# Two order edges on VectorE: the last Q clip behind an x addition, and a Q weight sum behind a K sink

## The chip, the cores and the metric

One Trainium2 chip, one of its cores. The time is device microseconds (us) of one execution. TensorE is called PE, VectorE DVE, ScalarE ACT, SyncE SP. A run counts as slow when it is over 1.5% above the fastest run of the same kernel; only fast runs are compared.

Each run also records the mean TensorE clock that was granted, as a share of full speed.

## The reference, cut to what matters

```python
# x: 2048 tokens x 1024, bf16; 32 heads of 32; MLP width 3584
q, k, v = heads(layernorm(x) @ wqkv)
phi = lambda t: where(t > 0, t + 1, exp(t)) + 1e-6
num, den = phi(q) @ (phi(k).T @ v), phi(q) @ sum(phi(k))
h   = x + (num / (den + 1e-6)) @ wo
n   = layernorm(h)
h2  = h + (relu(n @ W_gate) * (n @ W_up)) @ W_down
```

## The kernel before: the parts that matter here

The matrix products are split into seven block products each. DVE forms sums of weight blocks and of token blocks for this, PE multiplies, and DVE and ACT combine the results. The 16 token tiles go through the attention output one after another, and the first MLP products are interleaved with the last tiles, on tokens that are already finished. The stretch discussed here lies at 205 to 228 us.

The four sums of a weight, of which the Q weight's second is moved (the profile calls these lines L133 to L136):

```python
def sums():
    nc.vector.tensor_tensor(out=t1, in0=b12, in1=b11, op=ALU.subtract)
    nc.vector.tensor_tensor(out=t2, in0=b22, in1=t1, op=ALU.subtract)   # L134, moved
    nc.vector.tensor_tensor(out=t3, in0=b22, in1=b12, op=ALU.subtract)  # L135, needs no t2
    nc.vector.tensor_tensor(out=t4, in0=b21, in1=t2, op=ALU.subtract)
```

The end of the feature map `phi`: an Exp on ACT, then the clip (L217), which is moved, and a max, both on DVE:

```python
nc.scalar.activation(out=e, in_=dst, func=ACT.Exp, ...)
nc.vector.tensor_scalar(out=e, in0=e, scalar1=1.0, scalar2=PHI_EPS, op0=ALU.min, op1=ALU.add)
nc.vector.tensor_tensor(out=dst, in0=dst, in1=e, op=ALU.max)
```

A token tile's way through attention, with the names that the profile uses (line numbers of the kernel before):

```python
# nd: PE L527 -> PSUM; ACT takes the reciprocal; DVE writes three pieces of o_sb (L534)
# oT: a DMA transposes o_sb
# wo_h, for each half j:
#   PE attn L557;  DVE x_res L560: h = x + attn          <- "the x addition"
#   after both halves, ACT normalizes h into hn
nc.sync.dma_start_transpose(out=hnT[s][i][:, :, r:r + P], in_=st["hn"][:])   # hn_T, L581
# one step later, on DVE, the sums of the hidden state, L117 to L120, which read what that DMA wrote
left_sums(hnT[n // STS], hns[n // STS], slice(...), nc.vector)
```

Then PE multiplies hidden-state sums `hn`, `hs` by gate and up weight sums `tg`, `tu` (L733; the sums are L640, L644, L645, L646).

Of the kernel before, what the change touches and what calls it, by code (L numbers as in the profile page):

```python
# [7 lines left out]
ACT = mybir.ActivationFunctionType  # L8
ALU = mybir.AluOpType
# [6 lines left out]
PHI_EPS = 1e-6  # L16
# [15 lines left out]
def block_kernel(ctx: ExitStack, tc: tile.TileContext, x, wqkv, wo, wg, wu, wd, out, H: int):  # L32
    nc = tc.nc
# [10 lines left out]
    NW = 512  # L44
    NDW = P + HPC
    SW = 512
    NS = S // (2 * SW)
    KH = KC // 2
# [33 lines left out]
    negb = consts.tile([P, 2], FP32, name="negb")  # L82
# [39 lines left out]
    def left_ops(T, S):  # L122
        (a11, a12), (a21, a22) = blocks(T)
        s1, s2, s4 = (v[:] for v in S)
        return a11, a12, s4, a22, s1, s2, a21.bitcast(FP16)

    def right_ops(w, t):

        (b11, b12), (b21, b22) = [[w[:, k * KH:(k + 1) * KH, j * NW:(j + 1) * NW] for j in range(2)] for k in range(2)]
        t1, t2, t4, t3 = t[:, 0], t[:, 1], t[:, 2], b12.bitcast(FP16)  # L130

        def sums():
            nc.vector.tensor_tensor(out=t1, in0=b12, in1=b11, op=ALU.subtract)  # L133
            nc.vector.tensor_tensor(out=t2, in0=b22, in1=t1, op=ALU.subtract)  # L134
            nc.vector.tensor_tensor(out=t3, in0=b22, in1=b12, op=ALU.subtract)  # L135
            nc.vector.tensor_tensor(out=t4, in0=b21, in1=t2, op=ALU.subtract)  # L136

        return (b11, b21, b22, t4, t1, t2, t3), sums

# [66 lines left out]
    def phi_begin(dst, ps, m):  # L206

        if m is None:
            nc.scalar.activation(out=dst, in_=ps[:], func=ACT.Identity, bias=negb[:, 1:2], scale=1.0)
        else:  # L210
            nc.vector.scalar_tensor_tensor(out=dst, in0=ps[:], scalar=1.0 + PHI_EPS, in1=m,
                                           op0=ALU.add, op1=ALU.add)

    def phi_end(dst, e):

        nc.scalar.activation(out=e, in_=dst, func=ACT.Exp, bias=negb[:, 0:1], scale=1.0)
        nc.vector.tensor_scalar(out=e, in0=e, scalar1=1.0, scalar2=PHI_EPS, op0=ALU.min, op1=ALU.add)  # L217
        nc.vector.tensor_tensor(out=dst, in0=dst, in1=e, op=ALU.max)


    order = [(i * HS + s * SW) // P + tt for s in range(NS) for i in range(2) for tt in range(NT)]

# [4 lines left out]
    pspool = psctx.enter_context(tc.tile_pool(name="ps", bufs=1, space=PSUM))  # L227
    with ExitStack() as actx:
        apool = actx.enter_context(tc.tile_pool(name="apool", bufs=1))
        awork = actx.enter_context(tc.tile_pool(name="awork", bufs=2))  # L230
# [9 lines left out]
        def load_x(t):  # L240
            x_sb = bwork.tile([P, D], BF16, tag=("x_res", "oT")[atiles.index(t) % 2], bufs=XB, name="x_sb")
            nc.sync.dma_start(out=x_sb[:], in_=xf[t * P:(t + 1) * P, :])
            x_tiles[t] = x_sb
# [4 lines left out]
        def place(t):  # L248
            i, r = divmod(t * P, HS)
            s, r = divmod(r, SW)  # L250
            return s, i, r
# [13 lines left out]
        def ln_T(t):  # L265
            if t not in x_tiles:
                load_x(t)
            x_sb = x_tiles.pop(t)
            s, i, r = place(t)
            stats = asmall.tile([P, 2, nc.vector.BN_STATS_DIM], FP32, tag="stats", name="stats")  # L270
            for k in range(2):
                nc.vector.bn_stats(out=stats[:, k, :], in_=x_sb[:, k * NW:(k + 1) * NW])  # L272
            mv = asmall.tile([P, nc.vector.BN_AGGR_DIM], FP32, tag="mv", name="mv")
            nc.vector.bn_aggr(out=mv[:], in_=stats[:])
            sm = asmall.tile([P, 3], FP32, tag="sma", name="sma")
            lnv, rstd, nmr = (sm[:, k:k + 1] for k in range(3))
            nc.scalar.activation(out=lnv, in_=mv[:, 1:2], func=ACT.Ln, bias=LN_EPS, scale=1.0)
            nc.scalar.activation(out=rstd, in_=lnv, func=ACT.Exp, scale=-0.5)
            xn = bwork.tile([P, D], BF16, tag="hn", bufs=HB, name="xn")
            if t == atiles[0]:  # L280
                for k in range(2):
                    ks = slice(k * NW, (k + 1) * NW)
                    nc.vector.tensor_scalar(out=xn[:, ks], in0=x_sb[:, ks], scalar1=mv[:, 0:1], scalar2=rstd,
                                            op0=ALU.subtract, op1=ALU.mult)
                transpose_in(t, xn)
                return
            nc.vector.scalar_tensor_tensor(out=nmr, in0=mv[:, 0:1], scalar=-1.0, in1=rstd, op0=ALU.mult, op1=ALU.mult)
            nc.scalar.activation(out=xn[:], in_=x_sb[:], func=ACT.Identity, bias=nmr, scale=rstd)
            if t not in atiles[:PE_T]:
                nc.sync.dma_start_transpose(out=xT[s][i][:, :, r:r + P], in_=xn[:])  # L290
                return
            transpose_in(t, xn)
# [10 lines left out]
        rk, k_sums = right_ops(wk_sb, tk)  # L303
        rv, v_sums = right_ops(wv_sb, tv)
        pk, vs = {}, {}

        def token_unit(u, right, fin):

            s, _, r = place(units[u][0])
            left = left_ops(xT[s], xS[s])  # L310

            def mm(ps, m, v, start):
                for kc in range(KH):
                    nc.tensor.matmul(ps[:], lhsT=left[m - 1][:, kc, r + v * P:r + (v + 1) * P],  # L314
                                     rhs=right[m - 1][:, kc, :], start=(start and kc == 0),
                                     stop=(kc == KH - 1), skip_group_check=True)

            return strassen(pspool, awork, mm, fin)

        def new_pk(t):  # L320
            slot = atiles.index(t) % KC
            pk[t] = wo_mem[:, slot * D:(slot + 1) * D]

        def k_unit(u):
            ready = {}

            def fin(i, j, v, ps, m):
                t = units[u][2 * i + v]
                if not ready.get(t):
                    new_pk(t)  # L330
                phi_begin(pk[t][:, j * NW:(j + 1) * NW], ps, m)
                ready[t] = ready.get(t, 0) + 1
                if ready[t] == 2:
                    e = bwork.tile([P, D], BF16, tag="o_sb", name="e")
                    phi_end(pk[t], e[:])

            return token_unit(u, rk, fin)

        def k_plain(t):
            s, i, r = place(t)  # L340
# [52 lines left out]
        NU = len(units)  # L393
# [36 lines left out]
                    sums_unit(u + 1)  # L430
        sums_unit(0)
        rq, q_sums = right_ops(wq_sb, tq)
        q_sums()
        for t in units[-1]:
            kv_tile(t)
        nc.sync.dma_start(out=wo_sb, in_=wo.rearrange("(kc p) n -> p kc n", p=P))
        for c in range(KC):
            bnk, i = divmod(c, GPB)
            nc.vector.tensor_tensor(out=kvz[:, c, :], in0=kv_ps[bnk][:, i * NDW:(i + 1) * NDW],
                                    in1=mask[:], op=ALU.mult)  # L440
# [6 lines left out]
    def q_unit(s, c):  # L447

        left = left_ops(xT[s], xS[s])
        ready = {}  # L450

        def mm(ps, m, v, start):
            for kc in range(KH):
                nc.tensor.matmul(ps[:], lhsT=rq[m - 1][:, kc, (c + v) * P:(c + v + 1) * P],  # L454
                                 rhs=left[m - 1][:, kc, :], start=(start and kc == 0),
                                 stop=(kc == KH - 1), skip_group_check=True)

        def fin(i, j, v, ps, m):
            pair = pqT[:, j * KH + c:j * KH + c + 2, i * HS + s * SW:i * HS + (s + 1) * SW]
            phi_begin(pair[:, v], ps, m)  # L460
            if v == 1:
                e = qw[-1].tile([P, 2, NW], BF16, tag="e", name="e")
                phi_end(pair, e[:])

        return strassen(pspool, qw[-1], mm, fin, 3, s == NS - 1 and c + 2 == KH)

# [44 lines left out]
    held, added, squared = [], {}, {}  # L511
# [74 lines left out]
    STS = ST // NS  # L586
# [137 lines left out]
    quad_copies = [{} for f in range(NE)]  # L724
# [57 lines left out]
        attn_step(step)  # L782
    with tc.issue_after(added[order[STS], 0].ins):
        late_sums.pop()()
    steps = QSTEPS + STS + LAG[-1] - ready
    for n in range(steps):
        attn_step(ready + n)
        for p in flow[n * len(flow) // steps:(n + 1) * len(flow) // steps]:
            p()
    for t, copy in ((order[-2], ("m1", 1)), (order[-1], ("u3", 1))):  # L790
        tc.add_manual_dep(squared[t].ins, quad_copies[2][copy].ins.name,
                          mybir.DependencyInfo(mybir.DependencyClass.NoSync, mybir.DependencyReason.DATA),
                          reason="order")
    pqctx.close()
    psctx.close()
    abctx.close()
# [130 lines left out]
    for r, (wt, f, fi, toks) in enumerate(runs):  # L927
        w = [ops() for _, ops in now]
        later = []
        for n, s in enumerate(toks):  # L930
            first = n == 0 and isinstance(wt, int) and fi == 0
# [50 lines left out]
            if k == nwin - 3:  # L982
                for x in range(2):
                    t = wpools[1].tile([P, KC * 2 * GP * P], BF16, tag=("wg", "wu")[x], name="wd")
# [16 lines left out]
    for n in range(2):  # L1001
        t = fpool.tile([P, 4 * D], BF16, tag="wraw", bufs=2, name="xd")
# [247 lines left out]
    for n in range(1, len(OUTER)):  # L1250
        op = ops[n]
# [72 lines left out]
        else:  # L1324
            pss = []
            for p in range(4):
                ps = acc(("A", "A", "XY"[(n + 1) % 2], "XY"[n % 2])[p])
# [12 lines left out]
                s, t0 = divmod(2 * p, NT)  # L1340
                ts = slice(t0, t0 + 2)
                v = ps[:].rearrange("p (t d) -> p t d", t=2)
# [53 lines left out]
```

## Time and profile before

| | before |
|---|---|
| time, first three runs | 737.68 us (737.57 to 738.51) |
| span of the profiled run | 737.2 us (that run took 739.01 us) |
| PE busy in the span | 722.7 us |
| PE idle between 205 and 228 us | 1.94 us |

First the DVE timeline of the kernel before (start us, duration us, engine, line, operation; a bracket gives idle time ahead and what ended it):

```profile
214.95 0.42 DVE L640 TENSOR_TENSOR tg<-wg 128x512 f16<-128x512 bf16 x1
...
216.07 0.96 DVE L534 TENSOR_TENSOR o_sb<-nd,rd 128x384 bf16<-128x384 f32 x2
216.94 0.68 DVE L560 SCALAR_TENSOR_TENSOR x_res<-attn,x_res 128x512 bf16<-128x512 f32 x1
...
217.55 0.42 DVE L117 TENSOR_TENSOR hs<-hn 128x512 f16<-128x512 bf16 x1
```

Then SP's timeline of the DMA that feeds that L117, and the list of DMA issues of the stretch, whose last number is the median time in us from issue to landing:

```profile
213.02 1.23 SPq L581 DMA_TRANSPOSE hn<-hn  x1
```

```profile
hn<-hn SPq DMA_TRANSPOSE x1, 4.4
```

The transfer lands at about 213.02 + 4.4 = 217.4 us, and the sum that reads it starts at 217.55. It needed no wait, by about 0.1 us.

PE's timeline of the kernel before in the same stretch (start us, duration us, engine, line, operation; a bracket gives idle time ahead and what ended it):

```profile
216.62 0.75 PE L527 MATMUL nd<-kvz,pq_mem 128*128 128x132 bf16 x8
...
219.50 1.04 PE L733 MATMUL Aq<-hs,tg 128*128 128x512 f16 x4 [0.41 <-DVE tg L644]
...
221.83 3.40 PE L557 MATMUL attn<-wo_mem,oT 128*128 128x512 bf16 x14
```

`nd` of tile 12 runs through without a wait, and the next `attn` starts at 221.83 us.

### The profile page before, as it was taken

How to read it: one execution, taken by the hardware profiler on the slowest of the kernel's cores; microseconds unless marked ns; L12 is line 12 of the kernel's file. 1: busy time of each engine (PE TensorE's matmuls, PEld its weight loads, DVE VectorE, ACT ScalarE, POOL GpSimd, SP SyncE). 2: the span in 40 equal slices, each digit the busy share in tenths (PEclk: the TensorE clock that was granted, in tenths of full speed). 3: DMA queues.
4: the chain of work that ended last, by engine and by line, in shares of the span. 5: the costliest groups of instructions: out<-in, count | busy, mean ns of one | idle time of the engine just before them, and what ended most of it. 6: DMA issues, size and time to landing. Idle time of an engine off the chain costs nothing.

```text
span 737.2 us, 10549 instructions
## 1 busy us (share of the span) xinstructions
PE 722.7 (98%) x3967; PEld 381.8 (52%) x4020; DVE 556.0 (75%) x980; ACT 321.5 (44%) x580; POOL 20.7 (3%) x56
## 2 busy tenths in 40 slices
PE   8999999999989999999999999999999999999997
PEld 3444555444444444444444444444444458888667
DVE  6997644676789767688768787887786479996677
ACT  4776553778786655444344444443444120000000
POOL 0000000000000000000000000000000001100210
PEclk9999999999999999999999999999999999999999
DMA  9765002079977526175638358575483499978932
GB/s 315 169 145 157 0 1 95 21 168 230 215 166 166 135 73 208 43 207 135 196 106 243 114 188 270 182 219 193 162 280 120 137 392 343 305 253 283 257 44 58
DMA packets 143811, 128.88 MB, mean 175 GB/s; under 512 B 50960, under 2 KB 126096, under 8 KB 143760
## 3 DMA queue, kind: packets, MB, share of 16 engines
q1 hardware_dynamic: 136688, 123.30, 55.6%
q0 software_dynamic: 5312, 3.15, 3.4%
q10 hardware_dynamic: 1760, 1.77, 0.7%
q8 instruction: 31, 0.51, 0.3%
q14 instruction: 20, 0.16, 0.1%
HBM read 76.81 MB, written 39.85 MB: 158 GB/s over the span
## 4 chain that ended last, share of the span: by engine, by line
PE 85%; DVE 7%; DMA 4%; ACT 3%; issue 1%; SPq 0%; DVEq 0%; POOL 0%; ACTq 0%
PE accA L832 22%; PE accX L832 8%; PE accY L832 8%; PE accA L1167 8%; PE attn L557 6%; PE Aq L733 4%; PE Aq L314 3%; PE accA L993 3%; PE accX L1167 3%; PE Aq L454 3%; PE accY L1167 2%; PE Eq L314 2%; PE accY L993 2%; PE accX L993 2%; PE Eq L733 2%; DVE stats L272 1%
## 5 line engine op out<-in xcount | busy, mean ns | idle before, releaser
L842 ACT ACTIVATE gu<-gu 128x512 bf16<-128x512 bf16 x72 | 45.4, 630 | 131.3 <-DVE gu L841 131.3
L837 ACT COPY snap<-accA 128x1024 f32<-128x1024 f32 x72 | 72.5, 1008 | 36.5 <-PE accA L832 36.4
L832 PEld LDWEIGHTS <-tg 128*128 128x128 f16 x384 | 37.6, 98 | 45.3
L832 PEld LDWEIGHTS <-tu 128*128 128x128 f16 x384 | 37.6, 98 | 45.3
L557 PE MATMUL attn<-wo_mem,oT 128*128 128x512 bf16 x247 | 57.9, 379 | 2.6 <-DVE o_sb L534 1.3
L841 DVE TENSOR_TENSOR gu<-accY,snap 128x1024 bf16<-128x1024 f32 x36 | 43.9, 1219 | 10.0 <-ACT snap L837 10.0
L832 PE MATMUL accA<-hn,tg 128*128 128x512 f16 (+1 forms) x192 | 49.3, 379 | 0.0
L832 PE MATMUL accA<-hn,tu 128*128 128x512 f16 (+1 forms) x192 | 49.3, 379 | 0.0
L841 DVE TENSOR_TENSOR gu<-accX,snap 128x1024 bf16<-128x1024 f32 x36 | 43.9, 1219 | 6.4 <-PE accX L832 3.7
L154 ACT COPY u<-Aq 128x512 f32<-128x512 f32 x54 | 31.3, 581 | 36.6 <-PE Aq L314 19.3
L1167 PEld LDWEIGHTS <-x 128*128 128x128 f16 (+1 forms) x448 | 43.9, 98 | 5.5
L832 PEld LDWEIGHTS <-wu 128*128 128x128 bf16 x288 | 28.2, 98 | 34.0
L832 PEld LDWEIGHTS <-wg 128*128 128x128 bf16 x288 | 28.2, 98 | 34.0
L557 PEld LDWEIGHTS <-oT 128*128 128x128 bf16 x256 | 24.6, 98 | 32.5 <-issue 4.1
L845 DVE TENSOR_TENSOR hq<-gu 128x512 bf16<-128x512 bf16 x48 | 20.3, 423 | 14.3 <-ACT gu L842 14.2
L314 PEld LDWEIGHTS <-xT 128*128 128x128 bf16 (+1 forms) x192 | 18.6, 98 | 23.6 <-issue 2.3
L534 DVE TENSOR_TENSOR o_sb<-nd,rd 128x384 bf16<-128x384 f32 (+1 forms) x48 | 23.4, 508 | 8.3 <-ACT rd L533 6.1
L1131 POOL DMA_DIRECT2D out_dram<-o x12 | 15.2, 1265 | 508.8 <-DMA h<-h_dram 419.1
L1167 PEld LDWEIGHTS <-xs 128*128 128x128 f16 x280 | 27.4, 98 | 3.2
L560 DVE SCALAR_TENSOR_TENSOR x_res<-attn,x_res 128x512 bf16<-128x512 f32 x32 | 22.0, 686 | 8.6 <-PE attn L557 8.5
L1173 DVE TENSOR_TENSOR snap<-accA,u 128x1024 f32<-128x1024 f32 x16 | 19.5, 1221 | 11.4 <-PE accA L1167 11.3
L993 PEld LDWEIGHTS <-x 128*128 128x128 bf16 (+1 forms) x168 | 16.4, 98 | 19.6
(235 smaller groups left out, 1420.3 us busy)
## 6 DMA issues: line engine op xcount, KB each, us to landing
x<-x_dram SPq DMA_DIRECT2D x17, 896.0 KB, 8.8
x_dram<-hq SPq DMA_DIRECT2D x28, 512.0 KB, 3.2
wg<-in_B_W_gate_dram SPq DMA_DIRECT2D x14, 512.0 KB, 5.1
wu<-in_B_W_up_dram SPq DMA_DIRECT2D x14, 512.0 KB, 7.3
wraw<-in_B_W_down_dram SPq DMA_DIRECT2D x14, 512.0 KB, 4.9
x_dram<-hq SPq DMA_DIRECT2D x28, 256.0 KB, 2.7
t_dram<-wt SPq DMA_DIRECT2D x28, 256.0 KB, 2.2
xd<-x_dram SPq DMA_DIRECT2D x6, 896.0 KB, 6.9
```

The costliest lines, as they stand in the source:

```text
L154: copies[nm, v] = nc.scalar.copy(out=snaps[nm, v], in_=bank[v][:])
L314: nc.tensor.matmul(ps[:], lhsT=left[m - 1][:, kc, r + v * P:r + (v + 1) * P], rhs=right[m - 1][:, kc, :], start=(start and kc == 0), stop= ...
L454: nc.tensor.matmul(ps[:], lhsT=rq[m - 1][:, kc, (c + v) * P:(c + v + 1) * P], rhs=left[m - 1][:, kc, :], start=(start and kc == 0), stop=( ...
L534: nc.vector.tensor_tensor(out=ov[:, c0:c0 + n], in0=ndv[:, :, 0:P].rearrange("p k (h e) -> p k h e", h=HPC), in1=rd[:, 0:n, :].unsqueeze(3 ...
L557: nc.tensor.matmul(ps[:], lhsT=st["oT"][:, c, :], rhs=wo_sb[:, c, j * NW:(j + 1) * NW], start=(c == 0), stop=(c == KC - 1))
L733: nc.tensor.matmul(ps[:], lhsT=w(v, m)[:, kc, :], rhs=left[m - 1][:, kc, :], start=(start and kc == 0), stop=(kc == KH - 1), skip_group_ch ...
L832: nc.tensor.matmul(ps[:, v, :], lhsT=w[v][n - 1][:, kc, :], rhs=left[n - 1][:, kc, :], start=(t is not None and kc == 0), stop=(kc == KH - ...
L837: nc.scalar.copy(out=st[nm][:], in_=halves(st["A"]))
L841: add(out=g[:], in0=halves(st[nm]), in1=st[base][:], op=ALU.add)
L842: nc.scalar.activation(out=g[:, 0, :], in_=g[:, 0, :], func=ACT.Relu)
L993: nc.tensor.matmul(ps[:, t * NW:(t + 1) * NW], lhsT=x_tile(n, s, kh)[:, f, (t0 + t) * P:(t0 + t + 1) * P], rhs=w_tile(n, kh)[:, f, :], sta ...
L1167: nc.tensor.matmul(pv[:, tt, :], lhsT=left(m)[:, f, tt * P:(tt + 1) * P], rhs=right(m)[:, f, :], start=(t is not None and f == 0 and tt % ...
```

## The change

Two constraints for the instruction scheduler (order edges), no instruction more or less. A K unit is the set of seven block products that gives K for four token tiles; a sink is the DVE instruction (L211) that reads a finished product out of PSUM, where the matmuls of this program leave their results. The clip of the last pair of Q columns is to come after the first x addition of attention tile 8, because it made that addition wait. The second sum of the Q weight is to come after the first K sink of the last K unit, because it made an earlier sink wait.

```diff
+    def behind(late, first):
+        tc.add_manual_dep(late.ins, first.ins.name,
+                          mybir.DependencyInfo(mybir.DependencyClass.NoSync, mybir.DependencyReason.DATA),
+                          reason="order")
 ...
-        q_sums()
+        behind(q_sums(), k_begins[NU - 1, 0, 0, 0])          # q_sums returns its second sum
 ...
     with tc.issue_after(added[order[STS], 0].ins):
         late_sums.pop()()
+    behind(q_ends[NS - 1, KH - 2, 1, 0], added[order[STS], 0])   # phi_end returns the clip
```

The rest of the diff records the instructions that these two lines name, and uses `behind` where the same call stood written out.

## The prediction

> **What bounds the kernel now.** I read the page first, then PE's list of waits, then the timeline around the two instructions that the change moves, then the chain of waits there.

> ```profile
> PE 722.7 (98%) x3967; PEld 381.8 (52%) x4020; DVE 556.0 (75%) x980; ACT 321.5 (44%) x580; POOL 20.7 (3%) x56
> PE 85%; DVE 7%; DMA 4%; ACT 3%; issue 1%; SPq 0%; DVEq 0%; POOL 0%; ACTq 0%
> ```

> TensorE (PE) is busy 722.7 of 737.2 us, at full granted clock in all 40 slices, and holds 85% of the chain that ended last. All PE idle is 14.5 us. A change that only reorders VectorE (DVE) can win nothing but part of the idle time that DVE causes inside PE. PE's waits, longest first (total, times, longest):

> ```profile
> PE tp L299 <- DVE xT L300: 1.7, 1, 1.7
> PE attn L557 <- DVE o_sb L534: 1.3, 4, 0.5
> PE spin L400 <- DVE zero L397: 1.2, 1, 1.2
> PE attn L557 <- DVE x_res L560: 0.8, 1, 0.8
> PE nd L527 <- DVE o_sb L534: 0.5, 1, 0.5
> PE Dq L314 <- DVE wo_mem L211: 0.5, 1, 0.5
> ...
> PE Aq L733 <- DVE tg L644: 0.4, 1, 0.4
> ```

> Four of these lie near the moved instructions: `attn` behind the x addition (L560), `nd` behind `o_sb`, `Dq` behind a K sink (L211), and `Aq` behind a gate weight sum (L644). They fall at 212.02, 213.09, 72.26 and 219.50 us. Together they are 0.82 + 0.48 + 0.47 + 0.41 = 2.18 us, 0.3% of the time. That is about the ceiling for both edges.

> [...] the clip below stands 0.94 us at the head of DVE while an addition whose matmuls should be done stands behind it. [...] L134 took 1218 ns here, and it produces fp16 from bf16. [...] the trace has starts 1.13 us apart for two such sums of 1.22 us (L135 at 74.53, L136 at 75.66), so I use start-to-start distances. [...]

> **The change, part by part.** No instruction is added or removed. Each edge tells the instruction scheduler to place one DVE instruction after another on the same engine. The scheduler places instructions by its own estimate of times and by priority, so what it puts in the hole is the open question.

> *Edge A: the clip.* DVE before, with start, duration, instruction, and idle before it:

> ```profile
> 209.58 0.42 DVE L120 TENSOR_TENSOR hs<-hn,hs 128x512 f16<-128x512 bf16 x1
> 210.93 0.43 DVE L217 TENSOR_SCALAR e<-e 128x1024 bf16<-128x1024 bf16 x1 [0.94 <-ACT e L216]
> 211.28 0.69 DVE L560 SCALAR_TENSOR_TENSOR x_res<-attn,x_res 128x512 bf16<-128x512 f32 x1
> 211.88 0.09 DVE L560 DVE_READ_ACCUMULATOR x_res<-attn,x_res 128x1 f32 x1
> 211.88 0.69 DVE L218 TENSOR_TENSOR pq_mem<-pq_mem,e 128x1024 bf16<-128x1024 bf16 x1
> 212.49 0.55 DVE L534 TENSOR_TENSOR o_sb<-nd,rd 128x384 bf16<-128x384 f32 x1
> ```

> Counting the sixteen pairs of L560 in time order, the one at 211.28 is the first half of the ninth tile, index 8: just the one that the edge names. The clip ahead of it waits for an Exp that ScalarE started only at 209.76 (1.14 us long), because a Square and two copies came first. The matmuls of that half start at 207.59; eight at about 0.216 us end near 209.32, plus some 0.2 us to the wake-up. So the addition could start at about 209.92, straight after L120, and not at 211.28: 1.36 us sooner. Its result frees the PSUM buffer for which PE stands idle from 211.20 to 212.02. PE itself cannot use all of the 1.36 us: the 16 matmuls of tile 8 occupy it until about 207.59 + 16 x 0.216 = 211.04. The start at 212.02 can move to about 211.04.

> It then meets the next wait. The clip's Exp is still ready only at 210.93. If the clip and its max follow straight after the addition, clip 210.93, max 211.27, `o_sb` 211.87: all as before less the 0.61 us that the addition no longer spends behind the clip. So `nd`, which waits for `o_sb`, moves from 213.09 to about 212.48, and part of the 0.82 us reappears there: the two idles of 1.30 us become one of about 0.8 or 0.9. From 210.93 to past 219 DVE is nearly gapless (8.90 busy of 9 us from 211 to 220), so the whole queue up to L644 shifts by the same 0.6 us, and so does PE's start at 219.50. If other ready work fills the hole too, the shift can reach the full 0.94 us of removed stall; if L644 is also placed sooner, its 0.41 us is on top. After 219.50 PE is full to 249.4 and most of what it waits for is fed by PE itself, so the shift should stay. **Edge A: about 0.7 us gained** (0.6 plus a little for better filling).

> The late clip should harm nobody: the part of Q it completes is first read by the score matmuls of tile 12, which begin at 216.62, over 4 us later.

> *Edge B: the weight sum.* The Q weight's second sum (L134) now sits in the K unit before the last:

> ```profile
> 69.79 0.68 DVE L117 TENSOR_TENSOR xS<-xT 128x1024 f16<-128x1024 bf16 x1
> 70.39 1.22 DVE L134 TENSOR_TENSOR tq<-wq_sb,tq 128x2048 f16<-128x2048 bf16 x1
> 71.52 0.68 DVE L211 SCALAR_TENSOR_TENSOR wo_mem<-Dq,m 128x512 bf16<-128x512 f32 x1
> ...
> 72.26 1.02 PE L314 MATMUL Dq<-pq_mem,xT 128*128 128x512 bf16 x4 [0.47 <-DVE wo_mem L211]
> ```

> The sink L211 reads the single Dq buffer; PE needs that buffer for the other half and idles 0.47 us. The sink it is now put behind is that of the last K unit, at 96.84 us. There DVE idles for 1.90 us before 99.43, so L134 (1.13 us of queue) fits, and the fourth sum (L136), which needs it, can follow; at worst the second sink moves 0.3 us, which nothing reads at once. The Q unit needs these sums from 124.67 us on. So the destination is free, and the gain is 0.47 us or nothing, according to what takes the place. The third sum L135 is just as long (1.22 us), needs L133 but not L134, and no edge holds it. The trace has exactly such a swap: for the first up weight at 220.03 to 220.70 the order is L640, L645, L644, third sum before second. If L135 jumps into the hole at 70.39, the sink waits as before. I give 40% to the gap going: **0.2 us expected.**

> **Sum:** 0.7 + 0.2 = 0.9 us off 737.68, hence 736.8 us (-0.12%).

> **The rivals.**
> 1. *The clip edge only moves the wait.* Speaks for it: `nd` waits for `o_sb` a microsecond later, ScalarE gives its reciprocal only near 211.4, and ScalarE was busy 4.65 of the 5 us from 209 to 214. Against: DVE's stall is really removed and DVE has almost no slack behind it. Gain would be 0 to 0.3 us: about 737.4.
> 2. *Everything fills well:* all 2.18 us of the four waits go, 735.5. For: one queue feeds three of the four. Against: `nd` keeps its own wait, and the swap of L135 is likely.
> 3. *The third sum replaces the second* (edge B worth nothing): 737.0 with edge A as above. I think this slightly likelier than not.
> 4. *The schedule ripples.* An edge changes the scheduler's clock, so other instructions of PE, ACT and DVE can change places between 70 and 290 us. There are some 30 us of DVE-tight mixed work there, and one bad swap costs 0.4 to 1 us as the present gaps show. That could eat the gain: 737.7 to 738.5.
> 5. *DVE becomes the bound or a transfer is exposed:* DVE's work is unchanged at 75% and no load depends on either instruction by data; I give it nothing.

> **Range and chances.** The three runs of before span 0.94 us (737.57 to 738.51), as much as the effect. The low end, 735.6, is nearly all four waits gone; the high end, 738.0, is no gain with a small ripple or noise. Two per cent is 14.8 us, more than all of PE's idle time, so faster by 2% is nearly impossible; a loss that large would need a wholly new schedule. Faster 0.005, same 0.99, slower 0.005.

> **What would show it right or wrong.** Edge A is right if L560 of tile 8 starts within 0.3 us of the end of L120, ahead of the clip, PE's wait of 0.8 us for `x_res` is gone, `nd` still waits for `o_sb` for up to about 0.9 us, and the start after L644 is about 0.6 us sooner relative to the end of the preceding block. Edge B is wrong, in the way I expect, if L135 is found before the first sink of the earlier K unit and PE's 0.5 us for `wo_mem` L211 stays; right if that line vanishes. The prediction as a whole fails if PE's idle between 205 and 228 us (1.94 us before) does not fall, if new PE waits appear in other stages, or if PE's busy sum changes by over 1 us.

Its sum stands at 0.7 + 0.2 = 0.9 us off 737.68, hence 736.8. Two of its figures can be read from the trace of before: a row of 16 `attn` matmuls without a gap lasts 3.61 us, the last of them 0.38, so they follow each other at (3.61 - 0.38) / 15 = 0.215 us; and each of the eight x additions that waited for `attn` starts 0.19 to 0.20 us after 8 or 16 such steps of 0.216 us (the one at 179.27 us, for instance, in a row that began at 177.34), which is the "wake-up".

## The result, and the profile after

| | before | after |
|---|---|---|
| median of 6 runs | 738.26 us (737.57 to 739.62) | 740.86 us (739.29 to 741.15) |
| ratio of fast runs | 1 | 1.0029, 95% interval 1.0015 to 1.0043 |
| span of the profiled run | 737.2 us | 737.5 us |
| PE idle, 205 to 228 us | 1.94 us | 2.36 us |

A ratio is the mean time of one kernel's fast runs over that of the other's of the same rounds, so it is not quite the ratio of the medians. The change cost about 0.3%. That is small, within the two per cent of "same", but above the range on record.

PE's busy sum reads 724.8 us for after and 722.7 for before, with 4020 and 3967 matmul records; both traces hold 4020 weight loads and the program has the same matmuls, so the difference is one of recording, and the prediction's check by that sum says nothing.

PE's list of waits of the kernel after (total us, times, longest us):

```profile
PE nd L535 <- DVE o_sb L542: 1.3, 1, 1.3
...
PE Eq L741 <- DVE tg L648: 1.1, 1, 1.1
PE Dq L322 <- DVE wo_mem L211: 0.6, 1, 0.6
```

In this kernel the later lines named here are 8 further down (L527 is L535, L534 is L542, L557 is L565, L560 is L568, L640 is L648, L733 is L741), while L117 to L136, L211 and L217 keep their numbers. The wait of `attn` for `x_res`, 0.8 us in the kernel before, is gone, and so is the 0.5 us of `nd` at 213.09. The 1.3 us of `nd` is a new wait, at the next tile's `nd` (216.60 us), and `Eq` has a new wait of 1.1.

DVE's timeline of the kernel after:

```profile
208.75 0.42 DVE L120 TENSOR_TENSOR hs<-hn,hs 128x512 f16<-128x512 bf16 x1
209.42 0.69 DVE L568 SCALAR_TENSOR_TENSOR x_res<-attn,x_res 128x512 bf16<-128x512 f32 x1 [0.25 <-PE attn L565]
...
210.03 0.42 DVE L217 TENSOR_SCALAR e<-e 128x1024 bf16<-128x1024 bf16 x1
...
213.54 0.68 DVE L568 SCALAR_TENSOR_TENSOR x_res<-attn,x_res 128x512 bf16<-128x512 f32 x1
...
215.66 0.43 DVE L117 TENSOR_TENSOR hs<-hn 128x512 f16<-128x512 bf16 x1 [1.43 <-DMA hn<-hn]
216.00 0.88 DVE L542 TENSOR_TENSOR o_sb<-nd,rd 128x384 bf16<-128x384 f32 x2
...
218.53 0.42 DVE L648 TENSOR_TENSOR tg<-wg 128x512 f16<-128x512 bf16 x1
```

The top is as predicted: the x addition comes 0.25 us behind L120, and the clip follows it with no stall at all. The bottom is the surprise. The order was two pieces of `o_sb`, the x addition, L117; now L117 stands **ahead of** the two `o_sb` pieces. At the head of DVE it waits 1.43 us for its DMA, and the `o_sb` pieces wait behind it, though ACT had finished their reciprocals at 214.64 and 215.17 us. SP's timeline and the DMA issues of the kernel after:

```profile
212.03 1.46 SPq L589 DMA_TRANSPOSE hn<-hn  x1
```

```profile
hn<-hn SPq DMA_TRANSPOSE x1, 3.6
```

That transfer was issued 0.99 us sooner than before and took 3.6 us to land, against 4.4, so no slower DMA is the cause. The scheduler also put the first gate weight sum, L648, behind all this, at 218.53; it had been ahead of it.

What PE makes of it, in the timeline of the kernel after:

```profile
215.00 0.34 PE L535 MATMUL nd<-kvz,pq_mem 128*128 128x132 bf16 x3
216.60 0.33 PE L535 MATMUL nd<-kvz,pq_mem 128*128 128x132 bf16 x3 [1.27 <-DVE o_sb L542]
...
219.01 0.82 PE L741 MATMUL Eq<-hs,tg 128*128 128x512 f16 x3 [1.09 <-DVE tg L648]
...
221.85 3.40 PE L565 MATMUL attn<-wo_mem,oT 128*128 128x512 bf16 x15
```

At `nd` of tile 12, PE is 1.6 us ahead of the kernel before (215.00 against 216.62). Then come two idles of 1.27 and 1.09 us, and `attn` starts at 221.85 against 221.83. The lead is gone within 7 us.

The Q weight sum, in DVE's timeline and then PE's, of the kernel after:

```profile
70.54 1.22 DVE L135 TENSOR_TENSOR wq_sb<-wq_sb 128x2048 f16<-128x2048 bf16 x1
71.68 0.69 DVE L211 SCALAR_TENSOR_TENSOR wo_mem<-Dq,m 128x512 bf16<-128x512 f32 x1
```

```profile
72.42 1.02 PE L322 MATMUL Dq<-pq_mem,xT 128*128 128x512 bf16 x4 [0.62 <-DVE wo_mem L211]
```

The third sum took the place of the second, just as long, and the sink waits as before.

These two traces have spans 0.3 us apart, while the medians differ by 2.6 us. So one trace of each does not hold the whole loss; the profiled run of before, 739.01 us, was also slower than its three timed runs. The six runs of after say more: 739.29 and 739.38 us at a mean clock of 0.999 and 1.000, and 740.67 to 741.15 us at 0.997 or 0.998. There are two kinds of run, and the profiled one was of the quicker kind.

### The profile page after: what moved, and what is told of

Same layout as the page of the kernel before. It is cut to its first block, busy times and chain, and to the rows that moved or that the text cites. A ratio compares the mean times of both kernels' runs of the same rounds, so it can differ in the third digit from the quotient of the medians.

```text
span 737.5 us, 10604 instructions
## 1 busy us (share of the span) xinstructions
PE 724.8 (98%) x4020; PEld 382.0 (52%) x4020; DVE 556.3 (75%) x980; ACT 322.1 (44%) x580; POOL 20.7 (3%) x56
## 4 chain that ended last, share of the span: by engine, by line
PE 82%; DVE 8%; ACT 5%; DMA 3%; issue 1%; SPq 0%; DVEq 0%; POOL 0%; ACTq 0%
PE accA L839 22%; PE accY L839 8%; PE accX L839 8%; PE accA L1174 8%; PE attn L565 5%; PE Aq L322 3%; PE accA L1000 3%; PE accX L1174 3%; PE Aq L462 3%; PE accY L1174 2%; PE Aq L741 2%; PE Eq L322 2%; PE accY L1000 2%; PE accX L1000 2%; PE Eq L741 1%; DVE stats L280 1%
## 5 line engine op out<-in xcount | busy, mean ns | idle before, releaser
L565 PE MATMUL attn<-wo_mem,oT 128*128 128x512 bf16 x256 | 58.4, 379 | 1.3 <-DVE o_sb L542 1.3
L565 PEld LDWEIGHTS <-oT 128*128 128x128 bf16 x256 | 24.6, 98 | 31.4 <-issue 3.2
L542 DVE TENSOR_TENSOR o_sb<-nd,rd 128x384 bf16<-128x384 f32 (+1 forms) x48 | 23.2, 508 | 8.4 <-ACT rd L541 6.3
L568 DVE SCALAR_TENSOR_TENSOR x_res<-attn,x_res 128x512 bf16<-128x512 f32 x32 | 22.0, 687 | 8.7 <-PE attn L565 8.7
```

The source lines that it names most:

```text
L542: nc.vector.tensor_tensor(out=ov[:, c0:c0 + n], in0=ndv[:, :, 0:P].rearrange("p k (h e) -> p k h e", h=HPC), in1=rd[:, 0:n, :].unsqueeze(3 ...
L565: nc.tensor.matmul(ps[:], lhsT=st["oT"][:, c, :], rhs=wo_sb[:, c, j * NW:(j + 1) * NW], start=(c == 0), stop=(c == KC - 1))
```

## The experiments

All ran correctly, on four chips. Runs with the same number after the "e" shared a chip and the runs of the kernel before. PE idle is that between 205 and 228 us of the profiled run; the filling matmuls of the three kernels named warm count as busy.

| run | median us (range) | before in these rounds | ratio, 95% interval | PE idle |
|---|---|---|---|---|
| e1_none | 738.06 (737.60–739.93) | 738.50 | 1.0000 [0.9988, 1.0013] | 0.93 |
| e1_both | 739.75 (739.50–741.10) | 738.50 | 1.0022 [1.0009, 1.0034] | 3.02 |
| e1_clip_only | 741.79 (739.71–742.49) | 738.50 | 1.0042 [1.0028, 1.0056] | 3.49 |
| e1_q_only, 4 fast runs | 738.63 (737.85–740.30) | 738.50 | 1.0006 [0.9992, 1.0020] | profile slow |
| e2_stall_only | 740.59 (739.53–742.92) | 738.50 | 1.0028 [1.0012, 1.0044] | 2.81 |
| e2_clip_hsum | 738.44 (737.38–738.70) | 738.50 | 0.9992 [0.9979, 1.0005] | 1.22 |
| e2_warm | 740.20 (740.04–741.12) | 738.50 | 1.0023 [1.0009, 1.0037] | 1.79 |
| e2_both_fixed | 737.83 (737.22–742.08) | 738.50 | 0.9995 [0.9976, 1.0015] | 1.25 |
| e3_q_both | 738.33 (737.88–738.78) | 738.74 | 0.9990 [0.9976, 1.0003] | 1.62 |
| e3_fixed_again | 737.57 (737.08–738.98) | 738.74 | 0.9983 [0.9968, 0.9998] | 0.56 |
| e3_clip_again | 741.72 (739.69–743.90) | 738.74 | 1.0034 [1.0015, 1.0052] | 4.05 |
| e3_warm_again | 740.86 (739.89–742.76) | 738.74 | 1.0029 [1.0012, 1.0045] | 1.95 |
| e4_clip | 740.35 (739.38–740.94) | 738.39 | 1.0023 [1.0010, 1.0037] | 2.55 |
| e4_warm_more | 742.80 (742.23–744.36) | 738.39 | 1.0057 [1.0044, 1.0069] | 1.45 |

The theory: the clip edge makes the scheduler swap L117 with two pieces of `o_sb`, which exposes a transfer. The rivals: the Q edge does the harm; or the added code changes something else; or the difference is between chips or runs.

### e1_none, e1_both, e1_clip_only, e1_q_only: which part

The kernel after, with edges taken out:

```diff
-        behind(q_sums(), k_begins[NU - 1, 0, 0, 0])
+        q_sums()                                       # e1_none, e1_clip_only
-    behind(q_ends[NS - 1, KH - 2, 1, 0], added[order[STS], 0])
+    pass                                               # e1_none, e1_q_only
```

> The changed kernel with both edges taken out again, so the instruction order of the kernel before: a null test. Theory (the edges only reorder VectorE; the clip edge swaps a 0.94 us stall for a 1.43 us stall at the first hidden-state sum, the Q edge does nothing): ratio to before 0.999 to 1.001, same spread of spans and of granted clock as before. Rival (the slower runs at granted clock 0.997 come from the chip and not from the schedule): then this kernel shows some runs at 0.997 and about 739 us of span too.

> The changed kernel once more, beside its parts on one chip. Theory: the edges net to 0 to +0.3 us of PE idle, so at equal granted clock the span is within 0.5 us of before; ratio 1.000 to 1.001. Rival (the schedule itself costs 2 us or more[...]): ratio 1.002 to 1.004 again, with clock 0.997 in most runs of this kernel and not of the null test.

> Only the clip edge. Theory: all of what moves between 205 and 228 us comes from here: the 0.8 us wait for the x addition gone, a wait of some 1.4 us of VectorE on the DMA of the hidden-state transpose before the first hidden-state sum, PE waits for o_sb of some 1.3 us and for the gate weight sum of some 1.1 us; net 0 to +0.4 us. Rival (the slowdown is the clip edge's): ratio 1.002 to 1.004 here and 1.000 with the Q edge alone.

> Only the Q weight sum edge. Theory: the third sum takes the place of the second, so PE's wait of 0.5 us for the K sink stays and the time is that of before within 0.3 us (ratio 0.9995 to 1.0005). Rival (moving the second and fourth sum into the last K unit is what costs): ratio 1.002 or more and a new wait of PE between 94 and 125 us.

With no edge the code is as fast as before (1.0000), and the change repeats its loss on another chip (1.0022). The clip edge alone loses (1.0042), the Q edge alone neither wins nor loses (1.0006). One of its five runs, which was also the profiled one, was slow (761.67 us at a clock of 0.949) and is left out. So the loss belongs to the **clip edge**. The expectations of e1_both (at most 1.001) and e1_clip_only (a net loss of at most 0.4 us) missed; the ratios that their rivals gave, 1.002 to 1.004, came true or nearly so, though e1_both had only one of five runs at a clock below 0.999.

e1_none also corrects the reading of the kernel before. It has the same order of instructions in this stretch, yet its PE idles 0.93 us and not 1.94. The x addition starts at 209.85 us, 3.38 us after `nd` of tile 10 (206.47 us); in the first profile it was 211.28 less 207.04, or 4.24. PE has no wait for `x_res` at all. Of the four fast profiles without a clip edge, two show that wait (0.8 us in the kernel before, 0.6 in e3_q_both) and two do not (e1_none, e2_stall_only). The largest item that the prediction meant to win is there in some executions only. Counted from `nd` of tile 10, `attn` behind the stretch starts 14.79 us later in the kernel before, 14.82 in after and 13.94 in e1_none (206.47 to 220.41): against this execution, after loses 0.88 us here.

e1_clip_only was slower than e1_both, though it has less in it. Its trace shows why. PE's timeline, and two one-microsecond windows, of e1_clip_only (a window's columns: bounds, length, busy time and count of PE, PEld, DVE, ACT, POOL, then the granted PE clock, DMA share and GB/s):

```profile
219.92 1.46 PE L741 MATMUL Eq<-hs,tg 128*128 128x512 f16 x3 [1.09 <-DVE tg L648]
221.17 1.74 PE L741 MATMUL Aq<-hs,tg 128*128 128x512 f16 x4
```

```profile
220.00:221.00 1.00, 1.00 (x3) 0.35 (x4) 1.00 (x4) 0.97 (x9) 0.00 (x0) 0.50 1.07 319
221.00:222.00 1.00, 1.00 (x3) 0.30 (x2) 1.00 (x4) 1.00 (x1) 0.00 (x0) 0.50 0.51 156
```

Three `Eq` matmuls take 1.46 us where after's took 0.82, and the granted clock is 0.50. This was not in after's trace. It is the second kind of run, caught by the profile: from within the second idle on, PE works at half speed for 3.4 us.

### e2_stall_only, e2_clip_hsum: is it the swap

First the swap without the clip edge, then the clip edge without the swap, both without the Q edge. `o_parts` are the `o_sb` multiplications and `h_sums` the L117 sums, recorded where they are issued:

```diff
 # e2_stall_only: no edge of the change; tile 11's second o_sb piece behind tile 7's first hidden sum
-    behind(q_ends[NS - 1, KH - 2, 1, 0], added[order[STS], 0])
+    behind(o_parts[order[STS + 3], GPB], h_sums[STS - 1])
 # e2_clip_hsum: the clip edge, and that hidden sum kept behind tile 9's second x addition
     behind(q_ends[NS - 1, KH - 2, 1, 0], added[order[STS], 0])
+    behind(h_sums[STS - 1], added[order[STS + 1], 1])
```

> The order of the kernel before with one thing changed: the o_sb division of attention tile 11's second piece is put behind the first hidden-state sum of tile index 7, as the clip edge had brought about; neither edge of the change is there. Theory (the loss is this swap: VectorE then stands at the hidden-state sum until its DMA transpose has landed, and TensorE behind it): slower than before by 0.5 to 3 us, ratio 1.001 to 1.004, VectorE wait on the hidden-state DMA of over 0.5 us near 216 us. Rival (the loss comes from the clip itself or from other reorderings that came with its edge): within 0.3 us of before, ratio 0.9995 to 1.0005.

> The clip edge, plus an order edge that keeps tile 7's hidden-state sum behind the second x addition of tile 9, where the kernel before has it. Theory (the clip edge itself is sound, the swapped sum is what costs): no DMA wait of over 0.3 us before that sum, PE wait for o_sb back to 0.6 us or less, and 0.4 to 1.2 us faster than before: ratio 0.9985 to 0.9995. Rival (the clip edge costs by itself): ratio 1.002 or more again.

The swap alone costs 1.0028, as much as the whole change; its DVE order differs from that of e1_none in nothing else but one instruction of 0.2 us (L580), which comes behind L118 in place of ahead of it, as in after. DVE's and then PE's timeline of e2_stall_only:

```profile
217.78 0.42 DVE L117 TENSOR_TENSOR hs<-hn 128x512 f16<-128x512 bf16 x1 [1.96 <-DMA hn<-hn]
```

```profile
218.73 0.34 PE L535 MATMUL nd<-kvz,pq_mem 128*128 128x132 bf16 x3 [1.93 <-DVE o_sb L542]
```

The clip edge with the swap undone loses nothing (0.9992), and L117 no longer waits, in DVE's timeline of e2_clip_hsum:

```profile
216.86 0.42 DVE L117 TENSOR_TENSOR hs<-hn 128x512 f16<-128x512 bf16 x1
```

So the loss is shown to be the swap, from both sides. (The extra edge of e2_clip_hsum also brings L648 back ahead of the `o_sb` pieces; but in e2_stall_only L648 stays ahead, and the loss is as large.) e2_clip_hsum also shows what the clip edge is worth by itself: nothing that these runs can tell from zero. Its trace still has a wait of 0.66 us of `nd` for `o_sb` at 211.79 us, which is the prediction's first rival.

### e3_q_both: the Q edge made to work

```diff
-        behind(q_sums(), k_begins[NU - 1, 0, 0, 0])
+        [behind(op, k_begins[NU - 1, 0, 0, 0]) for op in q_sums()]   # second and third sum
-    behind(q_ends[NS - 1, KH - 2, 1, 0], added[order[STS], 0])
+    pass
```

> Only the Q edge, but with the third weight sum put behind the K sink as well, so that neither sum can stand before the sink of the earlier K unit. Theory: PE's wait for that sink falls from 0.4 to 0.8 us to 0.3 us or less (what is left would be the sink's own time), 0.2 to 0.6 us faster than before: ratio 0.9990 to 0.9998, within the noise of this method. Rival (the hole is filled by another instruction again): wait of 0.4 us or more stays.

The wait goes. PE's timeline of e3_q_both:

```profile
71.82 1.02 PE L322 MATMUL Dq<-pq_mem,xT 128*128 128x512 bf16 x4
```

There is no bracket: of the 0.47 us of idle ahead of it, 0.09 are left. The ratio, 0.9990, has an interval that includes 1, so the gain of about half a microsecond is seen in the trace and not established in the time.

### e2_both_fixed, e3_fixed_again: both edges, both mended

The edits of e2_clip_hsum and of e3_q_both's sums together.

> Both edges of the change mended: the hidden-state sum kept behind tile 9's addition, and the third Q weight sum put behind the same K sink as the second, so that nothing takes its place. Theory: PE's wait for the K sink (0.4 to 0.6 us) is gone and the x-addition wait too; 0.9 to 1.7 us faster than before, ratio 0.9977 to 0.9988. Rival (what PE wins is lost at the next wait): ratio 0.999 to 1.001.

> Both edges mended, a second time, because one of six runs stood 4 us above the others. Theory: median 0.5 to 1.2 us below before, ratio 0.9983 to 0.9993. Rival (no gain): ratio 0.9995 to 1.001.

The first set gave 737.83 us, but one run of six was 742.08 at a clock of 0.995, and the interval includes 1; the expected 0.9977 to 0.9988 was missed. The second gave 737.57 against 738.74, a ratio of 0.9983 with an interval just below 1, and PE idle in the stretch of 0.56 us. This is the fastest version. Its advantage over before is 0.7 and 1.2 us by the medians of the two sets, and only one of two sets confirms it.

### e2_warm, e3_warm_again, e3_clip_again, e4_clip, e4_warm_more: the half clock

The theory for the second kind of run: the longer idle of PE lets the clock fall. No run had shown it. It rests on e1_clip_only, where PE idles for 1.84 and 1.09 us, 2.93 us within 4.3, and in the second of these idles a dip to 0.50 begins, which is 3.413 us long in the trace's record of the clock. The rival: the dip has another cause and comes by chance. The test filled PE's idle with matmuls whose result is overwritten, beside the clip edge and without the Q edge:

```diff
-            for kc in range(KH):
-                nc.tensor.matmul(ps[:], lhsT=w(v, m)[:, kc, :], ...)
+            for kc in [0] * (6 if fc == 0 and m == 2 and v == 0 else 0) + list(range(KH)):
+                (fill if fc == 0 and m == 2 and v == 0 else []).append(nc.tensor.matmul(ps[:], ...))
 ...
+    behind(nds[order[STS + 4], GPB], fill[5]); behind(fill[0], nds[order[STS + 4], GPB - 1])
```

e4_warm_more adds five more for the second idle; e3_clip_again and e4_clip repeat e1_clip_only beside them.

> The clip edge alone, with six extra matmuls (1.3 us, their result is overwritten by the matmuls after them) put into the idle of PE before the score matmuls that wait for o_sb. Theory (the runs near 741.5 us are those in which PE's clock is halved for a few us because PE idled 2.4 to 2.9 us within 4.3 us): the granted clock stays at 0.999 or more, all runs fall to 739 to 740.3 us, ratio about 1.001 to 1.002, although PE does more work. Rival (the drop of clock is from chance or from elsewhere): most runs stay at 741 us or more, ratio 1.004.

> The clip edge alone again, now on one chip with the kernel that fills the idle. Theory (swapped sum plus, in most runs, a halved PE clock for some 3 us): at least half of the runs at 741.3 us or more, the rest near 739.7 us; ratio 1.003 to 1.005. Rival (the 741.8 us of the first time were that chip's): all runs below 740.5 us.

> The clip edge with six extra matmuls in PE's idle, on the same chip as the run above. Theory (PE's idleness is what halves its clock): no run above 741.2 us, median 1 us or more below that of the clip edge alone on this chip, though PE does 1.3 us more work. Rival: the same median as the clip edge alone, within 0.4 us.

> The clip edge alone, third time, as the reference on this chip for the run below. Expected again: at least half of the runs above 741.2 us, ratio 1.003 to 1.004.

> The clip edge with eleven extra matmuls (2.4 us, overwritten by the real ones), six in the idle before the score matmuls and five in the idle before the first matmul on a gate weight sum. Theory (idleness halves the clock): granted clock 0.999 or more in the trace, no run above 741.2 us, median 1 us or more below the clip edge alone, although PE does 2.4 us more work. Rival (the half clock is not from idleness): two groups of runs as before, median within 0.5 us of the clip edge alone or above it.

Several of these expectations missed. e2_warm kept its clock (0.999 or 1.000 in all five runs), but two of its five runs lay above the expected 740.3 us. e3_clip_again caught the dip again: the clock was 0.50 from 220 to 226 us, span 742.1. But e3_warm_again, with the idle filled, had two of six runs above 741.2 us, where none was expected; its median was 0.86 us below e3_clip_again's, where 1 us or more was expected. None of e4_clip's five runs was above 741.2, where half were expected. e4_warm_more ran at full clock (0.999 or 1.000) and was the slowest of all: the additional edges moved later matmuls too, and new waits of PE appear in its trace, 0.8 us of `Dq` for `gu` the longest. By time, the test is inconclusive.

Counting the clock of every run says more, though this count was not planned. A mean clock of 0.998 or less was recorded

- in 17 of 33 runs of kernels with the swap and no filling (after, e1_both, e1_clip_only, e2_stall_only, e3_clip_again, e4_clip),
- in 1 of 16 with the swap and PE's idle filled (e2_warm, e3_warm_again, e4_warm_more),
- in 5 of 30 fast runs of versions without the swap (e1_none, e1_q_only, e2_clip_hsum, e2_both_fixed, e3_q_both, e3_fixed_again), and in 3 of 40 of the kernel before beside these experiments.

So the half clock comes more often with the idle, and seldom where the idle is filled. That favours the idle as the cause.

```profile
215.78:219.19 3.41, 1.32 (x9) 0.58 (x8) 2.62 (x9) 2.01 (x5) 0.00 (x0) 1.00 0.73 171
219.19:222.60 3.41, 2.68 (x7) 1.03 (x8) 3.41 (x11) 3.01 (x9) 0.00 (x0) 0.50 0.93 246
```

```profile
213.94:217.35 3.41, 2.86 (x19) 1.48 (x18) 1.88 (x7) 2.92 (x10) 0.00 (x0) 1.00 1.08 175
217.35:220.76 3.41, 2.03 (x13) 0.97 (x12) 2.98 (x10) 2.01 (x7) 0.00 (x0) 1.00 0.63 158
```

In e2_stall_only the idle is cut in two by the edge of a window: 0.55 and 1.38 us. Where the edges fall differs from execution to execution, which would explain why only some runs of one kernel dip. This rule was found afterwards, ends of matmuls are modelled and some records are missing; and no profile caught a dip in a kernel without the swap, or in a filled one.

For the size, take the five kernels with the clip edge and the swap. Their 13 runs at 0.999 or 1.000 have a median of 739.71 us, their 14 others 741.35; the 37 runs at 0.999 or 1.000 of the kernel before have 738.50. **By these medians the stall costs about 1.2 us, and the half clock about 1.6 us more in half of the runs.** One window at half clock can cost at most 1.7 us, an estimate from its length of 3.413 us and the clock of 0.50.

## Why the prediction was wrong

The prediction said 736.8 us and at most 738.0; the time was 740.86.

**Edge A, up to the x addition: right.** The addition starts 0.25 us after the end of L120, within the 0.3 us named, the clip no longer stalls DVE (in e1_clip_only and e2_clip_hsum 0.33 us are left), and PE's wait for `x_res` is gone. The one idle of "0.8 or 0.9" us does not fit the prediction's own shift of 0.61, which leaves 1.30 less 0.61, or 0.69; e1_clip_only has 0.56 there and e2_clip_hsum 0.66, while after has none. The 1.3 us of `nd` in after lies at another tile and is no confirmation.

**Edge A, behind it: the step that failed.** It was this: "the whole queue up to L644 shifts by the same 0.6 us, and so does PE's start at 219.50". That takes the order of DVE behind the clip as fixed. The scheduler changed it. L117 moved ahead of two `o_sb` pieces, the `tg` sum moved back, and where a gain of 0.7 us was counted there is a stall of DVE of 1.43 us, and PE idles of 1.27 and 1.09. e2_stall_only and e2_clip_hsum show the swap as the cause.

**"A transfer is exposed … I give it nothing": wrong,** and for a reason that could be checked. It is true that no load depends on the clip by data. But a sum behind the clip reads a transfer that landed only 0.1 us ahead of it. In its old order it need not meet the transfer even when DVE is earlier: in e2_clip_hsum the sum starts 0.69 us sooner than before, at 216.86, and the transfer was issued sooner too and took less, landing at about 212.74 + 4.0 = 216.74 us. What exposed it is that the sum moved ahead of its neighbours.

**The fourth rival, the rippling schedule: right in kind, too small in size.** It gave "0.4 to 1 us" for a bad swap and 738.5 us at the most. The swap cost 1.2 us at full clock and came with the half clock, 1.6 us in half of the runs (17 of 33, against 5 of 30 without the swap), which no step of the prediction had.

**The size of the gain: too large.** The 0.82 us for `x_res`, the largest of the four waits summed to 2.18 us, was that of one execution; half of the profiles without the edge do not have it. With the swap undone, the clip edge gains nothing measurable (0.9992).

**Edge B: right in its third rival.** L135 took the place of L134, the wait stayed (0.47 us before, 0.62 after), and the destination was harmless. The 0.2 us expected from it is zero; the mended edge removes the wait from the trace.

**The base.** The starting median of 737.68 us is from three runs. Medians of before over all six runs and in the later rounds were 738.26 to 738.74, as much off as the effect that was predicted.

## What to carry to other kernels

An order edge fixes one pair of instructions and leaves the scheduler free with all others: list the order behind it anew before counting any gain, and if an instruction must not move up, give it an edge of its own. Before you make an engine earlier on which a waiting instruction holds up ready ones (here two `o_sb` pieces, whose reciprocals were done at 215.17 us, stood behind L117 until 216.00), compare the landing of each transfer with the start of its reader; where they lie 0.1 us apart, a reader that moves ahead of its neighbours waits (1.43 us here), while one that keeps its place need not (e2_clip_hsum). A wait of under a microsecond in one profile should be found in a second profile before it is worth a change.
